# VectorE's shrink moved ahead of the block transform that shares its tick

## The chip, the cores and the metric

The kernel runs on one core of one Trainium2 chip. The metric is device microseconds per execution. TensorE does the matrix products, VectorE and ScalarE read its results out of PSUM, GpSimd does some additions and issues some DMAs, SyncE issues most DMAs. Each engine runs its own queue strictly in the order in which the program issued it; semaphores order the engines against each other.

## The reference, cut to what matters

```
X  = rfft(x, axis=1)                       # x: 4 x 3008 x 256, float32
Yr = Xr @ w_r - Xi @ w_i + b_r
Yi = Xr @ w_i + Xi @ w_r + b_i
Y  = shrink(Yr) + 1j * shrink(Yi)          # sign(v) * max(|v| - 0.01, 0)
y  = irfft(Y, n=3008, axis=1).reshape(12032, 256)
h  = y @ w_in                              # 256 -> 2048
out = (h * sigmoid(h)) @ w_out             # 2048 -> 256
```

## The kernel before, in words

The 12032 tokens are cut into 24 blocks of 512 (the last one shorter), and the hidden width of 2048 into 16 slices of 128. A **tick** is one block with one slice. In tick t TensorE computes the first product of that slice (`mlp1`, line 599, six matmuls), and then the second product (`mlp2`, lines 757 and 761) for the slice of two ticks ago, whose activations ScalarE and VectorE split at the start of the tick before (`split_g`: `gh` by ScalarE, line 615, `gl` by VectorE, line 616). Numbers are kept as a high and a low part, so most products are three matmuls.

The transforms of the later batches are done beside these ticks, one piece per tick, from a list `fill` that a planner loop writes once: a key t holds what `fills(t)` issues after `mlp1`, a key t + 0.5 what is issued after the `mlp2` matmuls of that tick. The kinds of entry that matter:

- **mix** (`mix3`, lines 408 to 441): the complex product with w_r and w_i as three real ones. Its first product goes to one PSUM bank, which ScalarE copies out (`q`, line 421) and GpSimd adds the biases to (lines 422, 423); the other two go to a second bank `pv`. What VectorE then does with `pv` and `q` is the closure `shrink`: four additions or subtractions (line 434) that read `pv`, a clamp (line 437) and a subtraction (line 438), giving `y`. It is not issued in `mix3` but appended to the list `deferred`.
- **step** (`u3_step`): the second-stage transform `s2_3` (matmuls line 390), the split of an earlier `y` (`split_z`, lines 447 and 448) and the first inverse stage `i1` (matmuls line 462).
- **piece**: `stack_split` (ScalarE line 283, VectorE line 284), and one or two ticks later `stack_product`: two matmuls (line 293), each into a bank of its own, and a ScalarE copy and a VectorE addition for each (lines 294, 295).
- **block transform** (`i2` twice and `i2_ends` once per block): the last inverse stage (matmuls lines 524, 531), read from PSUM by `split_x`: ScalarE's copy of the high part (line 559) and VectorE's subtraction for the low part (line 563). `i2_ends` first splits what the block before left over in the tile `rest`, and at its end ScalarE copies a new `rest` out of the same bank (line 579). These banks are a pair with the tag "h", which `mlp1` uses too.

mix, step and piece draw their banks in turn from two tags of one bank each, `d0` and `d1` (`bank`): a bank is drawn again two draws later, and its first matmul waits until the readers of the tile before are done. A mix draws two: the bank of `q`, then `pv`. So in the next tick the second matmul of a `stack_product`, or the `i1` of a step that also has an `s2_3`, is on the bank of `pv`.

The planner puts 21 block transforms (blocks 3 to 9) between ticks 35 and 135. Where one shares its tick with a mix or a piece, it gets the key t + 0.5. Followed through, its loop gives such keys at ticks 35, 37, 40, 53, 57, 61, 67, 71, 83, 86, 93, 101, 104, 107, 115, 117, 122, 131, 133 and 135, all twenty with a mix, and at tick 77, with a piece. Those at 40, 61, 93, 107, 122 and 135 are `i2_ends`. The tick that follows has a `stack_product` in ten cases (41, 54, 58, 62, 68, 84, 87, 94, 105, 108) and a step in ten. The last entry of the list is in tick 148; blocks 10 to 22 run their first product by Strassen's scheme (line 680), from tick 160 on.

Of the kernel before, what the change touches and what calls it, by code (L numbers as in the profile page):

```python
# [149 lines left out]
def spectral_mlp_kernel(ctx: ExitStack, tc: tile.TileContext, x, w_r, w_i, b_r, b_i, w_in, w_out, c1, c2, c3, c4, c3f, c5, out):  # L150
# [43 lines left out]
    def flush(n):  # L194
        for dst, src in stores[:n]:
            nc.sync.dma_start(out=dst, in_=src)
        del stores[:n]
# [208 lines left out]
    deferred = []  # L406
# [185 lines left out]
    def mlp1(i, f):  # L592
        n = BLOCKS[i][1]
        h, l = xt[i]
        p = ps.tile([128, 512], F32, tag="h", bufs=2, name="h")
        m = 0
        for e in range(2):
            for w, v in ((win[0], h), (win[1], h), (win[0], l)):
                nc.tensor.matmul(  # L599
                    out=p[:, :n], lhsT=w[:, e, f * 128:(f + 1) * 128], rhs=v[:, e, :n],  # L600
                    start=(m == 0), stop=(m == 5),
                )
                m += 1
        g = sb.tile([128, 512], F32, tag="g", bufs=3, name="g")
        for q in halves(i, f):
            nc.scalar.activation(out=g[:, q], in_=p[:, q], func=ACTF.Silu)  # L606
        gf[i, f] = g

    def split_g(i, f):
        n = BLOCKS[i][1]  # L610
        g = gf[i, f]
        gh = sb.tile([128, 512], F32R, tag="gh", bufs=3, name="gh")
        gl = sb.tile([128, 512], F32R, tag="gl", bufs=3, name="gl")
        for q in halves(i, f):
            nc.scalar.copy(gh[:, q], g[:, q])  # L615
            nc.vector.tensor_sub(gl[:, q], g[:, q], gh[:, q])  # L616
        gf[i, f] = (gh, gl)
        units.extend((i, f, t) for t in range(n // 128))
# [71 lines left out]
    def fast_one(i, q):  # L690

        px = fast_bank()
        fast_product(px[:, 0:HB], i, q, 0, 0, True)
        fast_product(px[:, HB:BLK], i, q, 1, 1, False)
        fast.append([i, q, px])

    def fast_more():

        i, q, px = fast[-1]
        py = fast_bank()  # L700
        fast_product(py[:, 0:HB], i, q, (0, 0), (0, 0), True)
        fast_product(py[:, HB:BLK], i, q, 2, 2, False)
        u = tl.tile([128, HB], F32, tag="u", bufs=2, name="u")
        g = tl.tile([128, 4, HB], F32, tag="gp", bufs=3, name="gp")
        nc.scalar.copy(u, py[:, 0:HB])
        nc.vector.tensor_tensor(out=u, in0=px[:, HB:BLK], in1=u, op=ALU.add)
        nc.vector.tensor_tensor(out=g[:, 3, :], in0=px[:, 0:HB], in1=u, op=ALU.add)
        nc.vector.tensor_tensor(out=g[:, 3, :], in0=py[:, HB:BLK], in1=g[:, 3, :], op=ALU.add)
        fast[-1] += [u, py, g]

    def fast_two():

        i, q, px, u, py, g = fast.pop(0)
        fast_product(px[:, 0:HB], i, q, 3, (1, 1), False)
        nc.vector.tensor_tensor(out=g[:, 1, :], in0=px[:, 0:HB], in1=u, op=ALU.add)  # L715
        fast_product(py[:, 0:HB], i, q, (1, 0), (1, 0), False)
        fast_product(py[:, HB:BLK], i, q, (1, 1), 3, False)
        nc.scalar.activation(out=g[:, 1, :], in_=g[:, 1, :], func=ACTF.Silu)  # L718
        nc.scalar.activation(out=g[:, 0, :], in_=py[:, 0:HB], func=ACTF.Silu)  # L719
        nc.vector.tensor_tensor(out=g[:, 2, :], in0=py[:, HB:BLK], in1=u, op=ALU.add)  # L720

        def parts(r):
            h, l = [tl.tile([128, 2, HB], F32R, tag=f"g{k}", bufs=4, name=f"g{k}") for k in "hl"]
            v = g[:, 2 * r:2 * r + 2, :]
            if r:
                nc.scalar.activation(out=v, in_=v, func=ACTF.Silu)  # L726
            nc.scalar.copy(h, v)  # L727
            nc.vector.tensor_sub(l, v, h)  # L728
            gf[i, 2 * q + r] = tuple(a.rearrange("p a c -> p (a c)") for a in (h, l))
            units.extend((i, 2 * q + r, t) for t in range(BLK // 128))  # L730

        parts(0)
        later.append(lambda: parts(1))
# [114 lines left out]
    with tc.manual_schedule():  # L848
# [154 lines left out]
        fill = {}  # L1003
# [14 lines left out]
        def last_stage(i, first):  # L1018

            at(first - 2, i2_load, i)  # L1020
            put(first, i2, i, 0)
            put(first + 2, i2, i, 1)
            at(first + 2, i2_load, i, True)
            return put(first + 4, i2_ends, i)
# [29 lines left out]
        done, t, since = 37, 24, 0  # L1054
# [38 lines left out]
        for i in range(FAST[0], len(BLOCKS)):  # L1093
            if i in FAST:
                first = max(16 * i - 13, last + 1)
                t = last_stage(i, first)
# [19 lines left out]
        def fills(t):  # L1116
            for fn, args in fill.pop(t, []):
                fn(*args)
            if t == int(t):
                flush(1 if t < 12 else 4)  # L1120

        def run(n):
            for v in units[:n]:
                mlp2(*v)
            del units[:n]

        def rest_of_pair():
            while later:
                later.pop(0)()

        first_fast, last_fast = 16 * FAST[0], 16 * (FAST[-1] + 1)
        for t in range(len(ticks) + 1):
            i, f = ticks[t] if t < len(ticks) else (LAST, None)
            while deferred:
                deferred.pop(0)()
            if t and ticks[t - 1][0] not in FAST:
                split_g(*ticks[t - 1])
            if i in FAST:
                q = t - first_fast
                if f % 2 == 0:  # L1140
                    state["fast"] = True
                    fast_one(i, f // 2)
                    run(2)
                    if q:
                        fast_two()
                        run(2 if q > 2 else 0)
                else:
                    fast_more()
                    if f != 3:
                        rest_of_pair()  # L1150
                    run(2 if q < 4 else 4)
                    rest_of_pair()
                fills(t)
                continue
            if t == last_fast:
                run(2)
                fast_two()
                run(3)
                rest_of_pair()
            if f is not None:  # L1160
                mlp1(i, f)
            fills(t)
            if last_fast <= t < last_fast + 3:
                run(3 if t == last_fast else 4)
            else:
                run(sum(v[:2] != ticks[t - 1] for v in units))
            fills(t + 0.5)
        run(len(units))
        for k, (dst, src) in enumerate(stores):
            eng = nc.scalar if k % 2 else nc.sync  # L1170
# [28 lines left out]
```

## Time and profile before

| | us |
|---|---|
| median of 3 runs (1355.88 to 1358.32) | 1358.32 |
| the profiled execution | 1354.58 |
| its span, first to last instruction | 1352.7 |
| TensorE busy | 1323.8 (98%) |
| VectorE busy | 910.8 (67%) |
| ScalarE busy | 812.2 (60%) |
| GpSimd busy | 214.4 (16%) |
| mean granted clock of TensorE | 0.998 |

Matmuls are pipelined: the start of one stands less than its duration behind the start of the one before, so what a stretch of matmuls costs is read from start to start, not by adding durations.

### The profile page before, as it was taken

To read this page: it belongs to the slowest core of one execution; us is meant where nothing else is said; L and a number is where in the kernel's file an instruction comes from. 1 tells how busy PE (TensorE), PEld (TensorE's weight loads), DVE (VectorE), ACT (ScalarE), POOL (GpSimd) and SP (SyncE) were. 2 spreads that over 40 slices of the span, in tenths; PEclk is the share of its full clock that TensorE was granted. 3 is DMA by queue.
4 is the path that set the end of the run, shared out by engine and by line. 5 is a ranking of instruction groups with operands and counts; after the bars stand their busy time and mean duration, and the time that the engine had idled before them with its cause. 6 is when DMAs were issued, how large, how long until landed. Compare 5 with 4: busy or idle time off the path is not lost.

```text
span 1352.7 us, 22819 instructions
## 1 busy us (share of the span) xinstructions
PE 1323.8 (98%) x8437; PEld 1181.1 (87%) x8437; DVE 910.8 (67%) x1742; ACT 812.2 (60%) x1712; POOL 214.4 (16%) x322
## 2 busy tenths in 40 slices
PE   8989999999999999999999999999999999999998
PEld 4967888888888888888888999999999999999998
DVE  3867757777767777666667766666666666666663
ACT  5546555666656666555455666666666665666655
POOL 2001002222122221112112112111111111111100
PEclk9999999999999999999999999999999999999999
DMA  8875424454445453334210110011001100110000
GB/s 279 265 216 177 127 62 114 108 141 112 112 135 139 114 149 89 96 99 122 80 58 26 46 30 8 26 31 31 9 15 46 31 23 10 31 31 14 4 23 24
DMA packets 76124, 110.00 MB, mean 81 GB/s; under 512 B 8854, under 2 KB 54798, under 8 KB 76014
## 3 DMA queue, kind: packets, MB, share of 16 engines
q1 hardware_dynamic: 61895, 79.17, 20.1%
q0 software_dynamic: 10544, 25.68, 7.7%
q10 hardware_dynamic: 3575, 3.70, 0.9%
q8 instruction: 67, 1.10, 0.4%
q14 instruction: 43, 0.35, 0.1%
HBM read 71.03 MB, written 37.49 MB: 80 GB/s over the span
## 4 chain that ended last, share of the span: by engine, by line
PE 91%; DVE 3%; DMA 3%; ACT 1%; issue 1%; SPq 0%; ACTq 0%; DVEq 0%
PE acc L757 25%; PE h L680 19%; PE h L599 15%; PE acc L761 13%; PE mix L415 6%; PE s L390 2%; PE i L462 2%; PE mix L354 2%; PE i2e L531 2%; PE i L531 2%; DVE y L434 1%; PE s L293 1%; DMA scr<-s1o 1%; DMA scr<-i1o 1%; PE acc L752 1%
## 5 line engine op out<-in xcount | busy, mean ns | idle before, releaser
L757 PE MATMUL acc<-wout,gh 128*128 128x512 f32 x1472 | 539.8, 396 | 0.6 <-ACT gh L615 0.6
L761 PE MATMUL acc<-wout,gl 128*128 128x256 f32 x1472 | 413.6, 281 | 0.5 <-DVE gl L616 0.5
L757 PEld LDWEIGHTS acc<-wout,gh 128*128 128x128 f32 x1472 | 278.0, 189 | 48.0 <-ACT gh L615 0.8
L761 PEld LDWEIGHTS acc<-wout,gl 128*128 128x128 f32 x1472 | 277.1, 188 | 5.0 <-DVE gl L616 1.6
L599 PE MATMUL h<-xt,win 128*128 128x512 f32 (+1 forms) x1056 | 265.8, 387 | 0.0
L599 PEld LDWEIGHTS h<-xt,win 128*128 128x128 f32 x1056 | 181.4, 188 | 36.0 <-DVE xt L563 0.4
L606 ACT ACTIVATE g<-h 128x512 f32<-128x512 f32 (+1 forms) x177 | 102.0, 577 | 137.1 <-PE h L599 135.7
L728 DVE TENSOR_TENSOR gl<-gp,gh 128x512 fp32r<-128x512 f32 x208 | 148.6, 714 | 31.7 <-ACT gh L727 31.7
L718 ACT ACTIVATE gp<-gp 128x256 f32<-128x256 f32 x104 | 43.4, 417 | 176.8 <-DVE gp L715 176.8
L616 DVE TENSOR_TENSOR gl<-g,gh 128x512 fp32r<-128x512 f32 (+1 forms) x177 | 117.5, 664 | 41.3 <-ACT gh L615 39.7
L727 ACT CAST gh<-gp 128x512 fp32r<-128x512 f32 x208 | 129.0, 620 | 6.6
L680 PE MATMUL h<-xt,win 128*128 128x256 f32 x624 | 108.9, 283 | 0.2 <-DVE gp L715 0.2
L615 ACT CAST gh<-g 128x512 fp32r<-128x512 f32 (+1 forms) x177 | 106.0, 600 | 1.0
L720 DVE TENSOR_TENSOR gp<-h,u 128x256 f32<-128x256 f32 x104 | 44.2, 425 | 78.9 <-ACT gp L719 78.9
L680 PEld LDWEIGHTS h<-xt,win 128*128 128x128 f32 x624 | 88.6, 189 | 5.1 <-DVE gp L715 0.7
L680 PE MATMUL h<-th,sw_h 128*128 128x256 f32 x312 | 91.3, 293 | 0.0
L680 PE MATMUL h<-th,sw_l 128*128 128x256 f32 x312 | 88.4, 283 | 0.0
L680 PE MATMUL h<-tl,sw_h 128*128 128x256 f32 x312 | 87.7, 281 | 0.0
L422 POOL TENSOR_TENSOR q<-q,bias 128x256 f32<-128x256 f32 x36 | 28.0, 779 | 365.7 <-ACT q L421 365.7
L715 DVE TENSOR_TENSOR gp<-h,u 128x256 f32<-128x256 f32 x104 | 44.1, 424 | 55.0 <-PE h L680 54.8
L434 DVE TENSOR_TENSOR y<-q,mix 64x256 f32<-64x256 f32 x144 | 60.3, 419 | 22.6 <-PE mix L415 18.9
L726 ACT ACTIVATE gp<-gp 128x512 f32<-128x512 f32 x104 | 66.4, 639 | 0.0
(175 smaller groups left out, 2435.2 us busy)
## 6 DMA issues: line engine op xcount, KB each, us to landing
a<-scr SPq DMA_DIRECT2D x48, 256.0 KB
x_sb<-in_x_dram POOLq DMA_DIRECT2D x64, 188.0 KB, 3.9
gin<-scr SPq DMA_DIRECT2D x48, 192.0 KB
t<-in_c_dram POOLq DMA_DIRECT2D x36, 256.0 KB, 3.6
scr<-i1o SPq DMA_DIRECT2D x36, 256.0 KB
t<-in_c_dram SPq DMA_DIRECT2D x48, 128.0 KB
scr<-s1o SPq DMA_DIRECT2D x32, 192.0 KB
scr<-s1o SPq DMA_DIRECT2D x13, 384.0 KB
```

The source lines that it names most:

```text
L415: nc.tensor.matmul(out=out, lhsT=x_[:, e, c, :], rhs=m[:, e, :], start=(n == 0), stop=(n == 5))
L434: nc.vector.tensor_tensor(out=y[64 * i:64 * i + 64, r, :], in0=q[rows, i, :], in1=pv[rows, i, :], op=op,)
L599: nc.tensor.matmul(out=p[:, :n], lhsT=w[:, e, f * 128:(f + 1) * 128], rhs=v[:, e, :n], start=(m == 0), stop=(m == 5),)
L606: nc.scalar.activation(out=g[:, q], in_=p[:, q], func=ACTF.Silu)
L615: nc.scalar.copy(gh[:, q], g[:, q])
L616: nc.vector.tensor_sub(gl[:, q], g[:, q], gh[:, q])
L680: nc.tensor.matmul(out=p, lhsT=w[j], rhs=m[k], start=(begins and n == 0), stop=(n == 2), skip_group_check=True,)
L726: nc.scalar.activation(out=v, in_=v, func=ACTF.Silu)
L727: nc.scalar.copy(h, v)
L728: nc.vector.tensor_sub(l, v, h)
L757: nc.tensor.matmul(out=a, lhsT=gh[:, q], rhs=wout[:, f].rearrange("p a c -> p (a c)"), start=begins, stop=False,)
L761: nc.tensor.matmul(out=a[:, D:2 * D], lhsT=gl[:, q], rhs=wout[:, f, 0, :], start=False, stop=ends,)
```

## The change

Before, the entries of `deferred` are issued at the start of the next tick, ahead of `split_g`. So in a tick with a mix and a block transform VectorE's queue has the subtraction of `split_x` first and the shrink behind it. After, a tick that has a key t + 0.5 issues what is deferred ahead of that key: the shrink first, then `split_x`. No instruction is added or taken away, and no other engine's queue changes its order.

```
             else:
                 run(sum(v[:2] != ticks[t - 1] for v in units))
-            fills(t + 0.5)
+            if t + 0.5 in fill:
+                while deferred:
+                    deferred.pop(0)()
+                fills(t + 0.5)
         run(len(units))
```

## Rows read from the trace of the kernel before

**Rows 1.** The page, part 1: busy time, share of the span, instructions.
```profile
PE 1323.8 (98%) x8437; PEld 1181.1 (87%) x8437; DVE 910.8 (67%) x1742; ACT 812.2 (60%) x1712; POOL 214.4 (16%) x322
```

**Rows 2.** Waits of TensorE, whole span: waiter, releaser; total us, times, longest us.
```profile
PE s L293 <- DVE y L434: 11.3, 10, 1.3
...
PE i L462 <- PE s L390: 2.7, 6, 0.8
...
PE i L462 <- DVE zl L448: 0.5, 2, 0.3
```

**Rows 3.** Timeline of TensorE, tick 39: start us, us, line, operation, idle before.
```profile
238.72 0.63 PE L293 MATMUL s<-sx,c_sb 111*128 111x512 f32 x2
239.19 0.39 PE L757 MATMUL acc<-wout,gh 128*128 128x512 f32 x1
```

**Rows 4.** Timeline of TensorE, ticks 40 and 41.
```profile
244.01 0.28 PE L415 MATMUL mix<-ws,xl 128*128 128x256 f32 x1
...
247.89 0.40 PE L293 MATMUL s<-sx,c_sb 111*128 111x512 f32 x1
249.40 0.47 PE L293 MATMUL s<-sx,c_sb 111*128 111x512 f32 x1 [1.10 <-DVE y L434]
249.70 0.40 PE L757 MATMUL acc<-wout,gh 128*128 128x512 f32 x1
```

**Rows 5.** Timeline of VectorE, ticks 40 and 41.
```profile
247.09 0.41 DVE L563 TENSOR_TENSOR xt<-i2e,xt 128x242 fp32r<-128x242 f32 x1 [2.39 <-ACT xt L559]
247.53 1.72 DVE L434 TENSOR_TENSOR y<-q,mix 64x256 f32<-64x256 f32 x4
...
249.75 0.69 DVE L438 TENSOR_TENSOR y<-y,q 128x512 f32<-128x512 f32 x1
```

**Rows 6.** Timeline of TensorE, tick 44, a mix without a block transform.
```profile
262.23 0.28 PE L415 MATMUL mix<-ws,xl 128*128 128x256 f32 x1
```

**Rows 7.** Timeline of VectorE, tick 44.
```profile
262.62 1.72 DVE L434 TENSOR_TENSOR y<-q,mix 64x256 f32<-64x256 f32 x4 [0.88 <-PE mix L415]
```

**Rows 8.** Timeline of TensorE: the steps of ticks 34 and 36.
```profile
213.42 1.05 PE L390 MATMUL s<-t,a 128*128 128x128 f32 x8
214.23 0.36 PE L462 MATMUL i<-zh,t 128*128 128x256 f32 x1
...
223.25 1.05 PE L390 MATMUL s<-t,a 128*128 128x128 f32 x8
224.68 0.35 PE L462 MATMUL i<-zh,t 128*128 128x256 f32 x1 [0.38 <-PE s L390]
```

**Rows 9.** Timeline of VectorE, tick 36.
```profile
222.86 1.72 DVE L434 TENSOR_TENSOR y<-q,mix 64x256 f32<-64x256 f32 x4
```

**Rows 10.** Timeline of TensorE, ticks 107 and 109.
```profile
527.19 0.28 PE L415 MATMUL mix<-ws,xl 128*128 128x256 f32 x1
...
535.79 1.05 PE L390 MATMUL s<-t,a 128*128 128x128 f32 x8
```

**Rows 11.** Timeline of GpSimd, tick 107.
```profile
526.92 1.20 POOL L422 TENSOR_TENSOR q<-q,bias 128x256 f32<-128x256 f32 x1 [11.49 <-ACT q L421]
```

**Rows 12.** Timeline of VectorE, ticks 107 and 108.
```profile
527.45 0.97 DVE L563 TENSOR_TENSOR xt<-rest,xt 128x258 fp32r<-128x258 f32 x1
530.31 0.47 DVE L563 TENSOR_TENSOR xt<-i2e,xt 128x296 fp32r<-128x296 f32 x1 [1.90 <-ACT xt L559]
...
534.35 1.28 DVE L295 TENSOR_TENSOR s1o<-s,s1o 48x512 f32<-48x512 f32 x2
```

**Rows 13.** Timeline of ScalarE, ticks 107 and 108.
```profile
530.81 0.30 ACT L579 COPY rest<-i2e 128x174 f32<-128x174 f32 x1 [0.53 <-DVE xt L563]
...
532.16 0.58 ACT L294 COPY s1o<-s 48x512 f32<-48x512 f32 x1
```

**Rows 14.** Timeline of VectorE, tick 135.
```profile
651.29 0.73 DVE L563 TENSOR_TENSOR xt<-rest,xt 128x90 fp32r<-128x90 f32 x1 [0.30 <-ACT xt L559]
```

**Rows 15.** Timeline of GpSimd, tick 135.
```profile
651.17 0.73 POOL L422 TENSOR_TENSOR q<-q,bias 128x256 f32<-128x256 f32 x1 [8.40 <-ACT q L421]
```

## The prediction, made before the change was run

> **What bounds the kernel now.** I read the page's busy times first: TensorE is busy for 1323.8 of 1352.7 us, 98% of the span [rows 1], and no other engine passes 70%. So the time is TensorE's, and the change, which touches VectorE's queue alone, can act only through waits of TensorE. The second view is therefore the list of these waits over the whole span. Its largest entry is the one to see: the matmuls of `stack_product` (line 293) waited 11.3 us, ten times, for the shrink's additions (line 434). Below it stand six waits of `i1` (line 462), 2.7 us, put down to TensorE's own line 390, and two more for `zl`, 0.5 us [rows 2]. Ten is the number of block-transform ticks with a mix that are followed by a piece; six is the number followed by a step that has both an `s2_3` and an `i1`.
>
> The third view, the timeline, shows how a wait comes about. In tick 40 the last matmul of the mix starts at 244.01 and ends at 244.29 [rows 4]. VectorE begins the shrink only at 247.53, 3.24 us later, because the subtraction of `i2_ends` stands before it in the queue and waited for ScalarE until 247.09 [rows 5]. The four additions that read the bank `pv` end at 249.25, and TensorE, which had been at the first matmul of the pair at 247.89, starts the second at 249.40 [rows 4, 5]. In tick 44, a mix without a block transform, the shrink begins 0.11 us after the last matmul's end (262.23 + 0.28 = 262.51, then 262.62) [rows 6, 7]. The wait is queue order, not work.
>
> The six waits of `i1` look different in the list but are the same: in tick 36 the four additions run from 222.86 to 224.58 and `i1` starts at 224.68, 0.10 us later [rows 8, 9]. The profile names line 390, the last thing TensorE did; the bank is what was late.
>
> **What the change removes.** No instruction is added, removed or moved on TensorE, ScalarE, GpSimd or SyncE, and no DMA is moved. On VectorE six instructions pass one subtraction (two in an `i2_ends` with a `rest`), twenty times.
>
> - *The ten pieces.* An idle interval understates the price, since the pipeline of matmuls restarts after it. Undisturbed, the pair and the start of what follows take 239.19 - 238.72 = 0.47 us [rows 3]; in tick 41 they take 249.70 - 247.89 = 1.81 [rows 4]. The excess is 1.34 where the idle time is 1.10: add 0.24 to each wait. Ten waits: 11.3 + 10 x 0.24 = 13.7 us [rows 2 to 4].
> - *The six steps.* From the first `s2_3` matmul to the first `i1` matmul is 0.81 us undisturbed and 1.43 in tick 36 [rows 8]: excess 0.62 for a wait of 0.38, again 0.24 more. Six: 2.7 + 6 x 0.24 = 4.1 us [rows 2, 8].
> - *The two waits for `zl`.* `split_z` reads the `y` that the shrink leaves; these follow ticks 71 and 117, whose steps are the batch's last and have little before `split_z`. With the same restart: 0.5 + 2 x 0.24 = 1.0 us [rows 2].
>
> Together 18.8 us, if nothing takes their place.
>
> **Is the bank free early enough?** With the shrink at the head of the queue, tick 40 has it 0.11 us after the mix, at 244.40; four additions of 1.72 end at 246.12, and after a handover of 0.15 (249.25 to 249.40) the bank is TensorE's at 246.27 [rows 4, 5, 7]. TensorE wants it at 247.89 + 0.23 = 248.12 (the pair of 0.63 less one matmul of 0.40) [rows 3, 4]. That leaves 1.85 us. The wait goes entirely, and the next bank on the path is another.
>
> **What the change adds.** The subtraction of `split_x` now waits behind the shrink, 249.75 + 0.69 - 247.53 = 2.91 us from first to last [rows 5]. In the fourteen `i2` ticks ScalarE waits for nothing of this, the low part is needed a block later, and the bank of the tag "h" only when `mlp1` draws it two ticks on: cost nothing. In the six `i2_ends` ticks ScalarE's copy of the new `rest` starts only after VectorE's subtraction from the same bank: 530.81, after 530.31 + 0.47 [rows 12, 13]. Behind that copy ScalarE's queue holds `gh`, the activation of the next tick and the copies of `stack_product`, and a step two ticks after waits for the bank that these free.
>
> The worst of the six is tick 107, because there GpSimd is late: its first addition ends at 526.92 + 1.20 = 528.12, after the mix's end at 527.47 [rows 10, 11]. The shrink then runs from about 528.17 to 531.0 (I take 2.83, since its last subtraction overlaps the next operation's start a little). Behind it come the subtraction of `rest` and that of the transform.
>
> How long the one of `rest` takes is the open price. Beside GpSimd it took 0.97 for 258 columns, while the other, of 296 columns, took 0.47 [rows 12]; in tick 135 one of 90 columns took 0.73, to 652.02, just after GpSimd's addition ended at 651.90 [rows 14, 15]. So its length was set by GpSimd, and moved behind the shrink it runs alone: I take 0.45, after the row of 0.47, with 0.97 as the other end. Then VectorE is through at 531.9, the copy of `rest` begins at 531.95 instead of 530.81, 1.15 late, the first copy of `stack_product` at 532.16 + 1.15 = 533.3, ends at 533.9, and its addition (half of 1.28) frees the bank at 534.55, with the handover at 534.7 [rows 12, 13]. TensorE, 1.20 + 0.24 = 1.44 earlier by the wait removed (1.20 is that tick's own share of the 11.3), wants it at 535.79 - 1.44 = 534.35 [rows 10]. So 0.4 us comes back here, 0.9 with the long `rest`. In the other five GpSimd is not late by more than 0.1 us, and the same sum leaves nothing at 0.45. With the long `rest` everywhere, and all of ScalarE's delay (about 1 us each) on the path, it would be 6 us; none at all is the other end. I take 0.4.
>
> Two rules stand behind these rows. The Trainium skill ("PSUM — Partial Sum Buffer", section "PSUM bank collisions raise a hardware error") says that ScalarE and VectorE must not even read one bank at once, so the two reads have to be ordered; the 0.53 us that ScalarE waited in tick 107 agrees [rows 13]. Without it the copy of `rest` would pass the shrink and nothing would come back: 18.8. The skill's "SBUF — State Buffer" ("SBUF: two separate sides") says that a VectorE operation with two SBUF inputs and a GpSimd operation that reads SBUF exclude each other for a whole instruction. Tick 135 agrees, 0.73 for 90 columns [rows 14]. Were it wrong, the long `rest` would stay: 0.9 back, 17.9.
>
> **The sum.** 18.8 - 0.4 = 18.4 us off. The profiled execution took 1354.58, its span 1352.7 and 1.9 around it: it becomes 1336.2. The median of the runs is 3.7 above it, at 1358.32: 1339.9. TensorE remains the bound from tick to tick after tick 148, so what it gains stays gained; the next largest waits are in the prologue, which is not touched.
>
> **The rivals.**
>
> *Part of it comes back* (1343 to 1349). The same chain through ScalarE, but with slack used up after all ten pieces: for it speaks that the copies of `stack_product` keep their place behind a delayed ScalarE; against it that fourteen of twenty ticks have no `rest` and that the bank has 1.85 us to spare. At the 6 us of the upper end: 12.8 off, 1345.5.
>
> *The waits were not the queue's* (about 1358). If `pv` were held by something else, or the list `deferred` were empty at these places, the shrink would not move on the chip, or its wait be renamed. For it: the profile puts six of the waits on line 390. Against: 0.11 against 3.24 us between mix and shrink in two ticks that differ only by the block transform [rows 4 to 7].
>
> *Slower.* VectorE now stands at its queue's head until GpSimd has the biases added; before, the block transform covered that. If GpSimd came late in all twenty ticks, the shrink would start late by its whole delay with `split_x` and `gl` stuck behind. The point where it decides: before, the shrink began 3.24 us after the mix [rows 4, 5], so GpSimd must be later than that to lose. At 4.5 us the four additions end 4.5 + 1.72 + 0.15 = 6.4 after the mix, where TensorE comes at 248.12 - 244.29 = 3.8: a wait of 2.6, with restart 2.8 instead of 1.34 at ten pieces, and as much more at six steps: 16 x 1.5 = 24 us slower, 1382. Against it: 0.65 us in tick 107 [rows 10, 11].
>
> **How the numbers follow.** Forecast 0.77 (own range 1336 to 1343: both ends of the give-back, and the runs' spread of 2.4 us); part back 0.13; no change 0.07; slower 0.03. A change under 0.2%, 2.7 us, cannot be told from none. Faster 0.90, same 0.07, slower 0.03. The range reaches down to the median less 18.8 with that spread and up into the second case: 1334.5 to 1348.
>
> **What would show it.** Line 434 as releaser of line 293, and line 390 as that of line 462, vanish from TensorE's waits; the shrink starts 0.1 us after the mix in the twenty ticks (0.7 in tick 107); the pair of line 293 takes 0.47 us everywhere; ScalarE's copy of `rest` starts later by some tenths, by about 1.1 in tick 107; a short new wait of line 390 in tick 109. Wrong would be: the waits gone and the time unchanged, or new waits of `mlp1` or line 390 of more than 2 us together.

## The result, and the profile after

| | before | after |
|---|---|---|
| median of 4 runs, us | 1357.47 (1355.88 to 1358.32) | 1336.57 (1335.31 to 1340.42) |
| the profiled execution, us | 1354.58 | 1336.09 |
| its span, us | 1352.7 | 1334.2 |

The ratio is 0.9852, 95% interval 0.9829 to 0.9875: the change takes off 20.1 us, 17.0 to 23.2. The forecast was 1339.9 in a range of 1334.5 to 1348; for the profiled execution it was 1336.2, and that took 1336.09.

The page of the kernel after, part 1, has the same work in a shorter span [rows 1]:

```profile
span 1334.2 us, 22834 instructions
...
PE 1320.7 (99%) x8437; PEld 1182.2 (89%) x8437; DVE 907.5 (68%) x1742; ACT 811.4 (61%) x1712; POOL 215.0 (16%) x322
```

TensorE's waits in the kernel after, the whole list (waiter, releaser; total us, times, longest): no wait on line 434 is left, and none of line 462. Against [rows 2], all three entries are gone.

```profile
PE i L524 <- DMA gin<-scr: 2.7, 1, 2.7
PE s L333 <- DMA a<-scr: 2.1, 2, 1.2
PE warm L873 <- POOL zero L857: 1.4, 1, 1.4
PE s L257 <- DVE c L867: 1.0, 1, 1.0
PE acc L757 <- ACT gh L615: 0.6, 1, 0.6
PE i L531 <- DMA gin<-scr: 0.6, 1, 0.6
PE acc L761 <- DVE gl L616: 0.5, 2, 0.3
PE i L459 <- DMA t3f<-in_c3f_dram: 0.4, 1, 0.4
PE h L680 <- DVE gp L715: 0.2, 1, 0.2
```

Tick 40 and 41 of the kernel after, VectorE's timeline (start, duration, line, operation, idle before): the shrink now comes first and `split_x` behind it, the reverse of [rows 5].

```profile
243.47 1.72 DVE L434 TENSOR_TENSOR y<-q,mix 64x256 f32<-64x256 f32 x4 [0.67 <-POOL q L422]
245.22 0.43 DVE L437 TENSOR_SCALAR q<-y 128x512 f32<-128x512 f32 x1
245.68 0.69 DVE L438 TENSOR_TENSOR y<-y,q 128x512 f32<-128x512 f32 x1
246.29 0.48 DVE L563 TENSOR_TENSOR xt<-rest,xt 128x312 fp32r<-128x312 f32 x1
246.80 0.41 DVE L563 TENSOR_TENSOR xt<-i2e,xt 128x242 fp32r<-128x242 f32 x1
```

The shrink begins 0.11 us after the end of the mix in fifteen of the twenty ticks. In tick 53 it is 0.46, in ticks 86 and 107, where GpSimd is late, 0.7, and in ticks 37 and 101 it is 1.77, because VectorE is then still at `stack_split`'s subtraction (line 284). The prediction had 0.1 everywhere but in tick 107; none of these costs TensorE a wait.

And TensorE's there: the mix's last matmul, and the pair of `stack_product`, back to back, 247.43 - 246.96 = 0.47 us where [rows 4] had 1.81.

```profile
243.08 0.28 PE L415 MATMUL mix<-ws,xl 128*128 128x256 f32 x1
...
246.96 0.63 PE L293 MATMUL s<-sx,c_sb 111*128 111x512 f32 x2
247.43 0.39 PE L757 MATMUL acc<-wout,gh 128*128 128x512 f32 x1
```

The stretch that the change can touch runs from the first mix of the ticks to the last. The row of line 434 gives it by its first and last start: 504.7 us in the kernel before (first row), 485.9 in the kernel after (second row), 18.8 less. The columns are the duration's least, median and greatest in ns, then first and last start.

```profile
L434 DVE TENSOR_TENSOR y<-q,mix x144: 411/420/425, 199.4 to 704.1; 64x256 f32<-64x256 f32 x144
```

```profile
L434 DVE TENSOR_TENSOR y<-q,mix x144: 411/420/425, 199.8 to 685.7; 64x256 f32<-64x256 f32 x144
```

This number is free of the prologue, whose length varies from run to run (the first start of line 434 lies between 196.9 and 203.2 us in the traces of this case), and it serves below for every experiment. Behind the stretch nothing is given back: from the last start of line 434 to the end of the span it is 1352.7 - 704.1 = 648.6 us before and 1334.2 - 685.7 = 648.5 after.

### The profile page after: what moved, and what is told of

It is laid out like the page before. It is cut to its first block, busy times and chain, and to the rows that moved or that the text cites. A ratio compares the mean times of both kernels' runs of the same rounds, so it can differ in the third digit from the quotient of the medians.

```text
span 1334.2 us, 22834 instructions
## 1 busy us (share of the span) xinstructions
PE 1320.7 (99%) x8437; PEld 1182.2 (89%) x8437; DVE 907.5 (68%) x1742; ACT 811.4 (61%) x1712; POOL 215.0 (16%) x322
## 4 chain that ended last, share of the span: by engine, by line
PE 93%; DMA 3%; DVE 1%; ACT 1%; issue 0%; SPq 0%; POOL 0%; ACTq 0%; DVEq 0%
PE acc L757 25%; PE h L680 19%; PE h L599 16%; PE acc L761 13%; PE mix L415 6%; PE s L390 2%; PE i L462 2%; PE mix L354 2%; PE i L531 2%; PE i2e L531 2%; PE s L293 1%; DMA scr<-i1o 1%; DMA scr<-s1o 1%; PE acc L752 1%; PE i L459 1%; PE s L333 1%
```

## The experiments

Two theories stood against each other at first: TensorE waited for one bank, `pv`, held by the shrink's place in VectorE's queue; or all twenty ticks gain because VectorE's work is arranged better (less of it beside GpSimd's additions).

**The change in the ten ticks before a piece alone.**

```
             if t + 0.5 in fill:
-                while deferred:
+                piece = any(fn is stack_product for fn, _ in fill.get(t + 1, ()))
+                while deferred and piece:
```

> The change made only in the ten ticks that a stack_product follows; in the other ten the shrink stays behind the subtraction of split_x. Theory (the bank of pv, held by the shrink's queue place): the ten waits of line 293 go, with restart 13.7 us, less the 0.4 us that the kernel after shows as new in tick 109 (the start of line 390 and of its successor): 13.3 us under the kernel before, about 0.990 of it. The six waits of line 462, put down to line 390, and the two for zl stay, 2.7 and 0.5 us. Rival (every one of the twenty ticks gains alike, because VectorE's work no longer runs beside GpSimd's additions): half of the 20.1 us, 10 us, about 0.993, and the waits of line 462 shrink too.

Measured: 0.9898 (0.9876 to 0.992), 13.8 us off; its row of line 434 runs from 201.2 to 692.4, 491.2 us, 13.5 less than before. TensorE's list of waits still holds these two:

```profile
PE i L462 <- PE s L390: 2.7, 6, 0.8
...
PE i L462 <- DVE zl L448: 0.5, 2, 0.3
```

Line 293 is gone from the list, and the other two stand as they stood. 10 us, the rival's, lies outside the interval.

**The change in the ten ticks before a step alone** (the same edit with `not piece`).

> The change made only in the ten ticks that a step follows. Theory: the ten waits of line 293 stay at 11.3 us; the waits of line 462 go, 4.1 + 1.0 us with restart: 5.1 us under the kernel before, about 0.996. Rival (all twenty ticks alike): 10 us, 0.993, and line 293's waits get shorter. This and e1_pieces_only should add up to the whole change, 18 to 20 us, by the theory as 13.3 + 5.1.

Measured: 0.9965 (0.9947 to 0.9983), 4.7 us off; stretch 196.9 to 696.1, 499.2, 5.5 less. One entry of the three is left in TensorE's waits, to the digit:

```profile
PE s L293 <- DVE y L434: 11.3, 10, 1.3
```

The halves are 13.5 and 5.5, the whole 18.8: they add up to 0.2 us, each by its own waits. This also settles that the six waits which the profile puts on TensorE's own line 390 were the shrink's: they go with the shrink's place and with nothing else.

**VectorE's order as before, another bank for the second matmul.**

```
         for i in range(2):
-            p = bank("s1")
+            p = ps.tile([128, 512], F32, tag="h", bufs=2, name="s1") if i else bank("s1")
```

> The kernel before, with VectorE's queue as it was (shrink behind split_x), but the second matmul of stack_product on a bank of the pair with the tag h instead of the bank of pv. Theory (TensorE waits for the bank and for nothing else): the ten waits of line 293 go although the shrink is as late as before, 13.7 us under the kernel before, about 0.990; the shrink still begins 2.7 to 3.6 us after the mix. Rival (what VectorE does late, the shrink, gl and the additions of line 295, holds TensorE whichever bank it is): the second matmul or the next mlp1 waits about as long under another name, and the time stays within 3 us of before.

Measured: 0.9896 (0.9872 to 0.9919), 14.1 us off; stretch 201.5 to 692.6, 491.1, 13.6 less. In tick 40 VectorE's shrink is as late as ever, behind the transform (its timeline):

```profile
249.13 0.41 DVE L563 TENSOR_TENSOR xt<-i2e,xt 128x242 fp32r<-128x242 f32 x1 [2.40 <-ACT xt L559]
249.57 1.71 DVE L434 TENSOR_TENSOR y<-q,mix 64x256 f32<-64x256 f32 x4
```

and TensorE passes it all the same, 250.40 - 249.93 = 0.47 us for the pair (TensorE's timeline, tick 41):

```profile
249.93 0.63 PE L293 MATMUL s<-sx,c_sb 111*128 111x512 f32 x2
250.40 0.39 PE L757 MATMUL acc<-wout,gh 128*128 128x512 f32 x1
```

So in the ten ticks before a piece the late shrink cost nothing by itself. What cost was that the bank drawn next was the one it reads. The six waits of line 462 stay at 2.7 us in this run; another bank for `i1` was not tried.

**The subtraction of `rest` ahead of the shrink.** The kernel after shows the one loss that was forecast: in tick 109 the `mlp1` matmuls and the step's first one stand 1.70 us apart instead of 1.40 and `i1` follows after 0.91 instead of 0.81, 0.4 in all (TensorE's timeline of the kernel after):

```profile
518.49 1.57 PE L599 MATMUL h<-xt,win 128*128 128x512 f32 x6
520.19 1.16 PE L390 MATMUL s<-t,a 128*128 128x128 f32 x8
521.10 0.36 PE L462 MATMUL i<-zh,t 128*128 128x256 f32 x1
```

The next edits ask where it comes from.

```
         if i in rest:
             t = rest.pop(i)
             split_x(i, t, (slice(None), slice(None), slice(0, t.shape[-1])))
+        while deferred:
+            deferred.pop(0)()
...
-                while deferred:
+                while deferred and fill[t + 0.5][0][0] is not i2_ends:
```

> The kernel after, but in i2_ends the subtraction of rest goes ahead of the shrink, so that the queue is: rest, shrink, the transform's own subtraction. Theory (the 0.4 us in tick 109 come from the chain shrink, rest, transform, ScalarE's copy of rest, copies of stack_product): rest runs beside GpSimd again (0.73 to 1.0 us instead of 0.25 to 0.5) but ahead of the mix's end, ScalarE's copy of rest begins about 0.4 us earlier than in the kernel after, and the 0.4 us in tick 109 go; the time is that of the kernel after within 1 us, which no comparison can tell. Rival (GpSimd's lateness in tick 107 alone makes them): they stay.

Measured: 0.9868 (0.9843 to 0.9894), not to be told from the kernel after. The expected 0.4 us did not come in the tick that matters. VectorE was still busy with `gl` when tick 107's mix was done, and beside GpSimd `rest` took 0.97 us again, so the shrink began later and ScalarE's copy of the new `rest` 4.39 us after the mix instead of 4.47. The loss in tick 109 went from 0.4 to 0.3 us by the same reading of starts (1.62 and 0.91). The copy came 0.08 us earlier and the loss shrank by 0.08, which fits the chain, but it is too small to prove it; so I took ScalarE out.

**The copy of the new `rest` by VectorE.**

```
-            nc.scalar.copy(rest[i + 1], p[:, :, m:z])
+            nc.vector.tensor_copy(out=rest[i + 1], in_=p[:, :, m:z])
```

> The kernel after, with the copy of the new rest done by VectorE instead of ScalarE. e4_rest_first moved that copy by only 0.08 us in tick 107 (4.39 after the mix instead of 4.47) and the loss in tick 109 went from 0.39 to 0.31; this takes it out of ScalarE's queue. Theory (the loss comes through ScalarE, which stands behind VectorE's subtraction before it can go on to stack_product's copies): ScalarE waits for nothing in tick 107, the copies of line 294 begin about 1 us earlier after the mix, and from tick 108's mlp2 to line 390 and on to line 462 tick 109 has its usual 1.40 and 0.81 us; the time is that of the kernel after within 1 us, which no comparison tells. Rival (it comes through VectorE itself, whose additions of line 295 are late behind the shrink): the loss stays or grows by the copy's 0.2 us.

Measured: 0.9867 (0.9853 to 0.9882), again the time of the kernel after. Tick 109 is whole: 1.40 and 0.81 (TensorE's timeline):

```profile
519.60 1.57 PE L599 MATMUL h<-xt,win 128*128 128x512 f32 x6
521.00 1.05 PE L390 MATMUL s<-t,a 128*128 128x128 f32 x8
521.81 0.36 PE L462 MATMUL i<-zh,t 128*128 128x256 f32 x1
```

So the loss came through ScalarE. Its place in the queue, the copy of `rest` behind VectorE's read of the same bank, is what carried the shrink's move onto TensorE. It is too little to be told in the time.

**GpSimd made late.** The rival on the slower side said that the new order is lost once GpSimd's additions come later than 3.24 us after the mix. To try it, the first addition is repeated, in the twenty ticks alone, two or four times.

```
         nc.scalar.copy(q[:, 0, :], p[:, 0:D])
+        for _ in range(2 if state["shared"] else 0):
+            nc.gpsimd.tensor_tensor(out=q[:, 1, :], in0=q[:, 0, :], in1=bias[:, 1, :], op=ALU.add)
         nc.gpsimd.tensor_tensor(out=q[:, 1, :], in0=q[:, 0, :], in1=bias[:, 1, :], op=ALU.add)
...
+            state["shared"] = t + 0.5 in fill
             fills(t)
```

> The kernel after, with GpSimd's first addition of a mix done two times more before the real one (the same operands, the same value again), in the twenty ticks that have a block transform too. From the rows, 0.73 us and 0.08 between: the additions end 1.5 us after the mix instead of 0.15 before it, and the shrink starts at 1.5 instead of 0.1. Theory (TensorE meets the bank of pv 3.3 us after the mix where i2 stands between, 3.8 where i2_ends or the pair form does, and the four additions with their handover take 1.87): 3.4 against 3.3 to 3.8, so nearly nothing, but tick 86 and 107, where GpSimd was 0.65 late already, wait some 0.9 and 0.4; with restart 2 to 3 us over the kernel after, about 0.987 of the kernel before. Rival (the shrink's start has no margin, each microsecond that GpSimd is late is TensorE's): 20 x 1.4 = 28 us, slower than before.

> The same with four additions more: they end 3.1 us after the mix and the shrink starts there, about where it started in the kernel before (2.7 to 3.6). Theory: the four additions' bank comes 5.0 after the mix, against 3.3 (four ticks before a piece: 1.9 each with restart, and 2.7 in tick 87), 3.8 (1.5 in 68, 1.4 in 41, 62, 94, 2.2 in 108) and 3.9 to 4.4 (six steps: 7.5 together), and about 1 for the two waits of zl: 27 us over the kernel after, 6 us over the kernel before, 1.004 of it; the six waits of line 462 and the ten of line 293 are back. Rival (GpSimd's additions never reach TensorE's path): as the kernel after, 0.985.

Measured: 0.9937 (0.9925 to 0.995) with two and 1.0182 (1.0169 to 1.0195) with four: 8.5 us under and 24.7 us over the kernel before, where 18 under and 6 over were expected. The shrink starts as late as meant, about 1.5 and 3.1 us after the mix, in most of the twenty ticks; the price was another. TensorE's waits with two more additions show what had been left out:

```profile
PE s L390 <- DVE s1o L295: 2.7, 4, 0.7
...
PE h L601 <- ACT rest L581: 1.0, 3, 0.4
PE s L293 <- DVE y L436: 1.0, 3, 0.7
...
PE mix L415 <- DVE xl L402: 0.6, 2, 0.3
```

The bank of `pv` (line 293) costs 1.0 us of idle time, where 0.9 and 0.4 were expected. Beside it the same chain as in tick 109 now bites two ticks after each of the four `i2_ends` that a piece follows, 0.7 us each at line 390, and at `mlp1`, which draws the bank that ScalarE's copy of `rest` still reads. Tick 42 shows both, one after the other (TensorE's timeline):

```profile
253.29 1.66 PE L601 MATMUL h<-xt,win 128*128 128x512 f32 x6 [0.35 <-ACT rest L581]
255.63 1.16 PE L390 MATMUL s<-t,a 128*128 128x128 f32 x8 [0.69 <-DVE s1o L295]
```

With four, line 293 alone waits 14.8 us, and seven waits of `mlp1` have come to 5.6 (TensorE's waits):

```profile
PE s L293 <- DVE y L436: 14.8, 10, 2.3
...
PE h L601 <- DVE xt L565: 3.2, 3, 1.2
...
PE h L601 <- ACT rest L581: 2.4, 4, 1.1
```

**Late by two, with ScalarE out of the chain.**

```
+        for _ in range(2 if state["shared"] else 0):
+            nc.gpsimd.tensor_tensor(out=q[:, 1, :], in0=q[:, 0, :], in1=bias[:, 1, :], op=ALU.add)
...
-            nc.scalar.copy(rest[i + 1], p[:, :, m:z])
+            nc.vector.tensor_copy(out=rest[i + 1], in_=p[:, :, m:z])
```

> e5_gpsimd_late2 with the copy of the new rest done by VectorE, as in e7_rest_by_vector. e5_gpsimd_late2 lost some 10 us against the kernel after where 2 to 3 were expected; its waits name line 390 on line 295's additions (2.7 us, 4 times), mlp1 on ScalarE's copy of rest (1.0, 3 times) and line 293 on the shrink (1.0, 3 times). Theory (the second chain, shrink, rest, transform, ScalarE's copy of rest, stack_product's copies, has almost no margin, and only the pv bank was counted): with ScalarE out of it the first two go but for 0.1 or 0.2 us each, because VectorE's own queue is next; 3.7 us and seven restarts of 0.24, less up to 0.8: 4.6 to 5.4 us under e5, about 1341 or 0.990 of the kernel before. Rival (GpSimd's extra additions hold up VectorE's two-input operations, which is what costs): e5's loss stays, 0.994.

Measured: 0.990 (0.9883 to 0.9918), median 1341.1, as the chain through ScalarE would have it; the rival's 0.994 lies outside. That the time came out is in part luck, for the waits went only half as expected. Line 390's four are gone from the list, and so are the two of the mix's matmuls (line 415, 0.6 us above), which the expectation had not counted. But `mlp1`'s three stay, released by VectorE's copy now:

```profile
PE h L601 <- DVE rest L581: 1.0, 3, 0.4
PE s L293 <- DVE y L436: 0.8, 2, 0.7
```

That bank is held until `rest` is copied out of it, whoever copies.

TensorE has the same matmuls in the same order in all these kernels. So the delay of each against its twin in the kernel after, start by start, shows where the late GpSimd's time was lost (ticks 33 to 148, us over the kernel after):

| delay arises at | two additions | two, `rest` by VectorE | four |
|---|---|---|---|
| the pair of `stack_product`, `i1` and `mlp2` | 3.2 | 3.1 | 25.5 |
| `s2_3` (line 390) | 3.4 | -0.4 | 2.5 |
| mix, ticks 124 and 137 | 1.1 | 0.0 | 2.3 |
| `mlp1` (bank of the tag "h") | 1.9 | 1.9 | 7.4 |
| `mlp2` and `mlp1` at the lower clock | 0.0 | 0.0 | 4.6 |
| together | 9.6 | 4.6 | 42.4 |

The first line is what the two expectations had counted, the bank of `pv`, and it came close to them: 2 to 3 us with two additions and 27 with four. The next three lines were left out. Of the 7.4 us at `mlp1`, 3.9 fall in ticks 73, 117 and 119, each two ticks after an `i2`, where VectorE's delayed subtraction still reads the bank (line 565 in the list above).

The lower clock was left out too. With four additions TensorE's granted clock fell to the lower of its two levels, 1.2 GHz, in ticks 38 and 39, 87 and 88, and 108 and 109, behind waits of 1.92, 2.29 and 1.79 us, and rose again in the second tick of each pair. A wait of 1.80 us in tick 105 was not followed by a fall. In no other trace of this case does the clock fall between ticks 33 and 148. The same matmul takes 0.63 us there instead of 0.39 (TensorE's timeline with four additions, tick 38; the mean granted clock from 240 to 243 us is 0.54):

```profile
238.13 0.36 PE L464 MATMUL i<-zh,t 128*128 128x256 f32 x1 [1.92 <-issue]
...
238.92 0.39 PE L759 MATMUL acc<-wout,gh 128*128 128x512 f32 x1
...
240.43 0.63 PE L759 MATMUL acc<-wout,gh 128*128 128x512 f32 x1
```

## Why the prediction was right, step by step

*What bounds.* TensorE's waits were the right view: each of the three entries of [rows 2] went or stayed with its own ticks in the two half changes.

*The price of a wait.* The idle time of a stalled matmul is not its price. Taken tick by tick, from the first `mlp1` matmul of one tick to that of the next, the kernel before takes longer than the kernel after by 13.7 us in the ten ticks with a waiting pair, 4.1 in the six steps, 1.1 in the two that waited for `zl` and 0.3 in tick 124, and shorter by 0.4 in tick 109: 18.8 together. Forecast were 13.7, 4.1, 1.0, nothing and 0.4. So the 0.24 us that were added to each wait, from one pair and one step, hold for the pairs and steps as a whole: 13.7 - 11.3 is 2.4 over ten, 4.1 - 2.7 is 1.4 over six. Tick 124 is a wait that I left out: its eighteen mix matmuls, two ticks after an `i2_ends`, took 2.41 us from the first start to the start of `mlp2` in the kernel before and 2.15, like every other mix, in the kernel after and in the change before a step alone. No entry of the list of waits names it, and its cause is not shown.

*The bank's slack.* 1.85 us was worked out for tick 41. In the trace after, the four additions end at 243.47 + 1.72 = 245.19, with the handover of 0.15 at 245.34, and the second matmul starts at 246.96 + 0.23 = 247.19: 1.85. Hence the whole wait went.

*What the change adds.* 0.4 us in tick 109 was forecast and came, by the chain named. ScalarE's copy of `rest` starts 517.48 - 513.01 = 4.47 us after the mix in tick 107 against 530.81 - 527.47 = 3.34 [rows 10, 13], 1.13 later where 1.15 was forecast. The rows of the kernel after are TensorE's, then ScalarE's:

```profile
512.73 0.28 PE L415 MATMUL mix<-ws,xl 128*128 128x256 f32 x1
```

```profile
517.48 0.30 ACT L579 COPY rest<-i2e 128x174 f32<-128x174 f32 x1 [1.66 <-DVE xt L563]
```

The open price, `rest` away from GpSimd, was taken as 0.45: the same 258 columns took 0.97 us [rows 12] and take 0.42 (VectorE's timeline of the kernel after, tick 107):

```profile
516.53 0.42 DVE L563 TENSOR_TENSOR xt<-rest,xt 128x258 fp32r<-128x258 f32 x1
516.98 0.47 DVE L563 TENSOR_TENSOR xt<-i2e,xt 128x296 fp32r<-128x296 f32 x1
```

The Trainium skill's rule on the port that VectorE and GpSimd share ("SBUF — State Buffer", section "SBUF: two separate sides") is that, of a VectorE operation with two SBUF inputs and a GpSimd operation that reads SBUF, whichever starts first has it for the whole instruction. This trace agrees, 0.42 us away from GpSimd, and `rest` moved ahead of the shrink again showed the other side, 0.97 beside it.

*The sum.* 18.8 - 0.4 = 18.4 against 18.5 in the span and 18.8 in the transform stretch. That the profiled execution hit its forecast to 0.1 us is luck, since the prologue alone varies by more. The medians are 20.9 apart; the 2 us more lie inside the interval of the ratio, and no run shows where they come from. The range's lower end is not what its terms give as they are stated: the median less 18.8 less the spread of 2.4 is 1358.32 - 18.8 - 2.4 = 1337.1, and 1334.5 takes the spread about twice. The measured median, 1336.57, lies between the two.

*What was wrong.* The step on the slower rival: "GpSimd must be later than that to lose", that being 3.24 us. With GpSimd 1.5 us late the change keeps 8.5 us, with 3.1 it loses 24.7 (4.6 of them to the lower clock), both against the kernel before with GpSimd on time; a straight line between the two would put the point near 1.9, an estimate that no run tried. The kernel before with a late GpSimd was not run, so how the two orders compare under the same delay stays open. The step counted the bank of `pv` alone. The second chain, through ScalarE's copy of `rest`, had been worked out for tick 107 and found to cost 0.4 there, at a lateness of 0.65; that this chain has next to no slack in the ticks of `i2_ends` was thus worked out, and was not carried over to the rival. The bank of the tag "h" was taken to cost nothing, "only when `mlp1` draws it two ticks on". That holds for the change itself, where no wait of `mlp1` came, but with GpSimd 3.1 us late `mlp1` lost 7.4 us to it, 3.9 of them behind an `i2`.

## What to carry to other kernels

A wait on a PSUM bank is cured at either end: by serving the bank's reader earlier in its queue or by drawing another bank, and the second is the cheap proof that the bank was what counted. To price a stall, take start to start against an undisturbed repeat of the same stretch, not the idle time. And when an operation is moved ahead in a queue, look for what must now stand behind it on a second engine and for the banks that this holds, and work out their slack too. Here these, not the bank that was freed, took 6.4 of the 9.6 us lost with GpSimd 1.5 us late, and 12.3 of the 42.4 with it 3.1 us late.

## What the runs showed of the hardware

A stalled matmul cost 0.24 us more than its recorded idle time, at pieces and steps alike, while the mean granted clock was 0.998 before and 0.999 after, nearly all of it at the upper of TensorE's two levels, 2.4 GHz. Inside the transform stretch it fell to the lower one, 1.2 GHz, in the run with four additions alone, three times. VectorE and GpSimd hold each other up in both directions. `rest` took 0.97 us beside GpSimd and 0.42 away from it. And in tick 107 of the kernel after, GpSimd's first addition took 1.21 us instead of the 0.73 of [rows 15], beginning while VectorE was at `gl`, and the shrink waited for it (GpSimd's timeline, then VectorE's).

```profile
512.47 1.21 POOL L422 TENSOR_TENSOR q<-q,bias 128x256 f32<-128x256 f32 x1 [10.15 <-ACT q L421]
```

```profile
512.38 0.69 DVE L616 TENSOR_TENSOR gl<-g,gh 128x512 fp32r<-128x512 f32 x1
513.71 1.72 DVE L434 TENSOR_TENSOR y<-q,mix 64x256 f32<-64x256 f32 x4 [0.63 <-POOL q L422]
```
